# A fused attention, mixer and MLP kernel: a load pool planned by its real addresses, another rule for who gets the shared port, and the first loads issued from two queues

## The chip, the cores and the metric

The kernel runs on one core of one Trainium2 chip. The core has a matrix engine (PE, with its weight load shown as PEld), a vector engine (DVE), an activation engine (ACT), a general engine (POOL) and a queue engine (SP) that here only issues DMAs; ACT issues some as well. The metric is the device time of one execution in microseconds (us). The kernel before took 1355.23 us, the median of three runs between 1351.61 and 1355.76.

## The reference

Three parts follow each other on eight batches of 576 tokens and 512 features. First a linear attention with 8 heads of 64: `k` and `q` are projected by `w_phi` to 128 features, the row maximum of the absolute values is taken off, and both signs go through an exponential.

```
phi(x):  p = x @ w_phi; p -= max|p|; return [exp(p), exp(-p)]
kv = phi(k)^T v;  z = sum phi(k);  x = (phi(q) kv) / (phi(q) z + 1e-6)
```

Then a gated mixer and, at last, a Fourier mixing with a layer norm and an MLP:

```
gate = sigmoid(causal conv of 5 taps over x);  val = x @ w_val
x = (gate * val) @ w_out
u = x + Re(fft over tokens (fft over features (x)))
un = (u - mean) / sqrt(var + 1e-6)
out = u + max(un @ w_ch1, 0) @ w_ch2        # 512 -> 2048 -> 512
```

All inputs are fp32 but for the weights of the mixer and the MLP, which are fp64 bit patterns converted on the chip.

## The kernel before, in words

**Precision.** A product in nearly full fp32 is made of three fp32r products (`mm3`, lines 109 to 113): each operand is split into a high part (ACT, `hi_act`) and the rest, the low part (`lo_dve` on DVE or `lo_pool` on POOL). So most tiles cost one ACT and one DVE or POOL instruction. DVE and POOL read SBUF over a port that they share.

**Stages.** The attention (about 0 to 310 us) is written in a fixed order by hand (`run_attention`): 16 units of two batches by two heads, five groups each. `load_kq` and `load_v` bring a unit in; the first unit's `k` and `q` come in three pieces each. From then on a planner sets the order. `note_mix` (some 310 to 640 us) and `note_mlp` (to the end) only note operations with what they read and write; `place_ops` gives each a due time, then places them one after the other, always the one that can start first on its engine, and emits the result as five parts in time.

**The mixer**, batch by batch b = 0 to 7: `note_x` splits the attention's output `x`, `note_taps` makes the convolution and gate, `note_V` multiplies by `w_val` (PE `val`, then DVE `gv` and `gs`, then the split `ge`). `note_W` multiplies by `w_out` for four feature blocks c in the order 0, 2, 1, 3 (PE `ps<-ge,wo`, 96 matmuls for a batch). The parts are kept in `x2` (`x2b` for the last batch), and for c = 2 and 3 the difference `fs` is split into `f` (high part on ACT, low part on POOL). `note_FD` is the Fourier product over features (PE `ps<-ft,f`, result `Y` and `rem`), `note_SD` that over tokens (PE `ps<-sq,Y`), after which `u` goes to DRAM (`u_scr`). Here W(7), FD(5) and so on name such a step of batch 7 or 5.

**The MLP** works on five blocks of tokens of two halves of 462. A one-level Strassen scheme needs seven operand tiles `un` (0 to 6, each a high part `un,i,0` and a low part `un,i,1`) and seven sums of each weight, which POOL makes in the tile `ws` beforehand (`note_sums`, 16 steps). The ring `r0` (10 tiles) and `r1` (6) hold weights on their way from DRAM (`s_scr`). Three PE products per step write banks `x`, `y`, `z` and two others, `cx`, `cy`, collect the second layer in `acc`.

**The crossing from mixer to MLP.** The first block's layer norm is done during the mixer (`ln0`, in the tile `A`: two halves, three steps each) and stored to `un_scr0` and `un_scr1`. `load_first` loads the four parts from there into the low tiles of `un` 0, 6, 2 and 1, and `prep_un` (from line 795) makes the rest by subtractions on DVE or POOL (`A<-un,un` is the first, from `un` 6 and `un` 0). The tiles `un`, `r0`, `c11`, `c12`, `c22` stand in a pool (`open_mlp`) over memory that other pools held before. The list `LX` (lines 564 and 565) is their order in memory; `OLD` (from line 567) is the planner's table of what held that memory and what must be done first; `over` looks a tile up in it. The waits that the program really makes come from the addresses, not from that table.

**The port in the planner.** `free["x"]` is the time from which the shared port is free. An operation that may run on DVE or POOL ("vp") is offered to POOL unless line 1239 forbids it.

Of the kernel before, what the change touches and what calls it, by code (L numbers as in the profile page):

```python
# [13 lines left out]
ACTF = mybir.ActivationFunctionType  # L14
# [51 lines left out]
def attention_moe_mixer_kernel(  # L66
# [163 lines left out]
    def load_kq(u):  # L230
        t = P["g1"].tile([128, 2, 2 * S], F32, tag=f"g{u % 2}", name="kqraw")
        cuts = (0, 256, 640, 2 * S) if u == 0 else (0, 2 * S)
        for c0, c1 in zip(cuts, cuts[1:]):
            for w, src in enumerate((k, q)):
                nc.sync.dma_start(out=t[:, w, c0:c1], in_=src[u, :, c0:c1])
        raw[u] = [t]

    def load_v(u):
# [305 lines left out]
    def seq_pass(p, main, rem, a):  # L544
# [5 lines left out]
        else:  # L550
# [10 lines left out]
    ops = []  # L561
    ring = None

    LX = [("un", 3, 0), ("un", 3, 1), ("un", 4, 0), ("un", 4, 1), "c11", ("un", 0, 1), ("un", 6, 1), "c12", ("un", 0, 0), ("un", 6, 0), ("un", 1, 0),
          ("un", 2, 0), ("un", 5, 0), ("un", 5, 1), "c22"] + [("r0", i) for i in (3, 4, 5, 6, 7, 8, 9, 0, 1, 2)] + [("un", 2, 1), ("un", 1, 1)]
    LX_SHAPE = {"un": [2, HB], "r0": [2, 2, 128], "c11": [HB], "c12": [HB], "c22": [HB]}
    OLD = [(8192, [("done", "V", n) for n in range(2)])] * 2 + [(4 * (S + 4) * 4, [("done", "x", b)]) for b in (NB - 2, NB - 1)]
    OLD += [(4 * S * 4, OLD[0][1])] * 2 + [(4 * S + 8 * NE + 16 * NE + 8 * S - 4 * S, [("done", "g", m) for m in (2, 3)])]
    OLD += [(16 * 4 * NE, [("done", "W", c, a) for c in range(4) for a in range(2)])]

    def over(*tiles):

        keys = []
        at = 0
        for t in LX:
            n = LX_SHAPE[t if isinstance(t, str) else t[0]]
            size = -(-4 * n[0] * (n[1] if len(n) > 1 else 1) * (n[2] if len(n) > 2 else 1) // 64) * 64
            if t in tiles:
                o = 0
                for m, k in OLD:  # L580
                    if o < at + size and at < o + m:
                        keys += [x for x in k if x not in keys]
                    o += m
            at += size
        return keys
# [364 lines left out]
    def note_W(b, c):  # L950
        gh, gl = (later(("ge", b % 2, k)) for k in range(2))
        w = int(b == NB - 1)
        t = later(("x2", w))
        fs, f = tl["fs"], [later(("f", i)) for i in range(2)]
        for a in range(2):
            k, p = next(ring)
            p = p[:, 0:NE]

            def prod(e, a=a, p=p):
                for kk in range(4):  # L960
                    ws = slice(c * 128, (c + 1) * 128)
                    mm3(p, (wo[0][:, kk, ws], wo[1][:, kk, ws]), (gh[:, kk, a], gl[:, kk, a]), kk == 0, kk == 3)
            op("m", 0, prod, [("ge", b % 2, kk, i) for kk in range(4) for i in range(2)] + ["wo"], [k] + [("done", "W", c, a)] * (b == NB - 2), 12 * 0.134)
            if c >= 2:
                o_tt("v", fs[:, a], t[:, c - 2, a], p, (ALU.add, ALU.subtract)[a], NE, [k, ("x2", w, c - 2, a)], [("fs", a)])
            if c == 2 and a == 0:
                r = later(("xr", b % 2))
                o_hi(r[0:1], p[0:1], NE, [k], [("xr", b % 2, 0)])
                o_lo("v", r[32:33], p[0:1], r[0:1], NE, [k, ("xr", b % 2, 0)], [("xr", b % 2, 1)])
            o_act(t[:, c, a], p, ACTF.Copy, NE, [k], [("x2", w, c, a)])  # L970
        if c >= 2:
            c0 = c - 2
            fk = [("fs", 0), ("fs", 1)]
            o_hi(f[0][:, c0], fs, 2 * NE, fk, [("f", c0, 0)])
            o_lo(K["t_lo"], f[1][:, c0], fs, f[0][:, c0], 2 * NE, fk + [("f", c0, 0)], [("f", c0, 1)])
        if c == 2:
            q0 = 32 * (b % 4)
            o_act(later("r256")[q0:q0 + 1], t[0:1, 2], ACTF.Copy, 2 * NE, [("x2", w, 2, 0), ("x2", w, 2, 1)], [("r256", b % 4)])
# [79 lines left out]
    def note_mix():  # L1058
        rings = [[(("ps", i), later(("ps", i))) for i in range(n)] for n in (4, 5)]
        nonlocal ring  # L1060
        ring = cycle(rings[0])
        sums = iter(range(len(wsteps)))
        SUMS = [(1, 0, 1, 0, 1)] * 5 + [(1, 0, 0, 0, 0), (0,) * 5]

        def add_sums(n):
            for i in range(n):
                k = next(sums, None)
                if k is not None:
                    in_place(note_sums, k)

        ln0 = chain(ln_first(0), ln_first(1))
        tail = note_tail()
        next(tail)
        for m in range(4):
            note_taps(0, m)
            note_V(0, m)
            next(tail, None)
        for b in range(NB - 1):
            note_x(b + 1)
            for i, c in enumerate((0, 2, 1, 3)):  # L1080
                if i < 3:
                    note_taps(b + 1, i)
                    note_V(b + 1, i)
                note_W(b, c)
                add_sums(SUMS[b][i])
            add_sums(SUMS[b][4])
            note_taps(b + 1, 3)
            note_V(b + 1, 3)
            if b == NB - 2:
                ring = cycle(rings[1])  # L1090
                break
            note_FD(b)
            note_SD(b)
            for k in range((0, 1, 1, 2, 1, 1, 0)[b]):
                in_place(next, ln0, None)
        drain(ln0)
        b = NB - 2
        for n in range(RING[0]):
            note_weights(0, n)
        load_first()  # L1100
        note_FD(b)
        for c in (0, 2, 1, 3):
            note_W(b + 1, c)
        note_SD(b)
        note_FD(b + 1)
        note_SD(b + 1)
        prep_un(0, K["un0"])
# [30 lines left out]
    def place_ops():  # L1138
# [89 lines left out]
        for _ in range(n):  # L1228
            best = None
            for e, q in ready.items():  # L1230
                cand = []
                for i in q:
                    d = ops[i][0]
                    if any(left_by[e][:max(part[i], at_part[e])]):
                        continue
                    t = first(i, e)
                    if e == "p" and "v" in d:
                        ahead = sum(ops[j][0]["v"] for j in ready["v"] if j != i and due[j] <= due[i] and at[j] <= t + 0.5)
                        if t + d["p"] > max(max(free["v"], at[i]) + ahead + d["v"], due[i] + behind + d["v"] - K["marg"]):
                            continue  # L1240
                    cand.append((i, t))
                if not cand:
                    continue
                t0 = min(t for i, t in cand)
                i, t0 = min(((i, t) for i, t in cand if t <= t0 + K["win"]), key=lambda c: (due[c[0]], c[0]))
                if best is None or t0 < best[0]:
                    best = t0, e, i
            t0, e, i = best
            for q in ready.values():
                q.discard(i)  # L1250
            part[i] = at_part[e] = max(part[i], at_part[e])
            for j in succ[i]:
                part[j] = max(part[j], part[i])
            for k in ops[i][0]:
                left_by[k][last[i]] -= 1
            free[e] = t0 + ops[i][0][e]
            if e == "p" or e == "v" and ops[i][5]:
                free["x"] = free[e]
            if e == "a":
                table = ops[i][8] or table  # L1260
            if e == "m":
                behind = t0 - due[i]
            start[i], end[i] = t0, free[e] + ops[i][4]
            if ops[i][10]:
                free["w"] = max(free["w"], free[e]) + K["bw"] * ops[i][10]
                end[i] = free["w"] + K["dl"]
            order.append((i, e))
            for s in succ[i]:
                at[s] = max(at[s], end[i] + lat * ("m" not in ops[i][0] or "m" not in ops[s][0]))
                left[s] -= 1  # L1270
                if not left[s]:
                    enter(s)
# [141 lines left out]
            place_ops()  # L1414

    if True:
        nc.vector.memset(eps, 1e-6)
        nc.scalar.activation(out=warm, in_=eps, func=ACTF.Exp)
        nc.sync.dma_start(out=wp[0:64], in_=w_phi)
        nc.sync.dma_start(out=wp[64:128], in_=w_phi)  # L1420
        load_kq(0)
        nc.sync.dma_start(out=ident, in_=ident_in)
        load_v(0)
        nc.vector.memset(f32(ones), 1.0 / DM)
# [104 lines left out]
```

## Time and profile before

| what | value |
|---|---|
| median of three runs | 1355.23 us |
| the profiled execution, its own time | 1354.46 us |
| its span, first to last instruction | 1352.7 us |
| PE busy | 1307.7 us, 97% |
| DVE busy | 1178.4 us, 87% |
| ACT busy | 918.9 us, 68% |
| POOL busy | 822.2 us, 61% |

The span is what the instructions cover; 1.76 us of the execution's time lie around it. A busy share is a mean over stages: PE may be full in one and wait in the next. In the table of stretches the column PEclk is the clock granted to the matrix engine as a share of full speed; 1.00 is 2.4 GHz and 0.50 the lower level of 1.2 GHz, on which a matmul takes twice as long and the engine still counts as busy.

### The profile page before, as it was taken

Reading aid. Unit: us, or ns where it says so; the run is one execution under the profiler, and the core shown is the slowest. Engines: PE = TensorE matmul, PEld = TensorE weight load, DVE = VectorE, ACT = ScalarE, POOL = GpSimd, SP = SyncE. Lnnn points to the kernel's source line nnn. Section 1 sums busy time; section 2 is a strip of 40 time slices with the busy share of each in tenths; the row PEclk is TensorE's granted clock in tenths of the full one; section 3 lists DMA queues with packets and bytes.
Section 4 is the critical chain, followed back from the end, with each engine's and each line's share of the span. In section 5 each row is a group of like instructions: output and inputs, shape, how many; then the busy total and the mean of one; then the engine's idle time right before and its main releaser. Section 6 shows DMA issues by size and latency. Waiting matters only on the chain.

```text
span 1352.7 us, 30778 instructions
## 1 busy us (share of the span) xinstructions
PE 1307.7 (97%) x11952; PEld 1193.7 (88%) x11952; DVE 1178.4 (87%) x1867; ACT 918.9 (68%) x1872; POOL 822.2 (61%) x653
## 2 busy tenths in 40 slices
PE   7899999998999999989999999999999999999998
PEld 7788888987999999988888888888888888888997
DVE  6989988889898999869988999899988978998775
ACT  6888888866455555555877676776778676766662
POOL 4979798805666655525555765677657866673431
PEclk9999999999999999989999999999999999999999
DMA  7488888643343333243733473347333653346332
GB/s 255 143 267 263 285 280 298 209 175 130 126 141 134 127 126 133 96 154 125 236 103 106 134 231 104 102 134 237 104 108 105 211 160 102 107 112 204 103 90 87
DMA packets 151598, 214.63 MB, mean 159 GB/s; under 512 B 16790, under 2 KB 112278, under 8 KB 151452
## 3 DMA queue, kind: packets, MB, share of 16 engines
q1 hardware_dynamic: 147216, 203.21, 47.1%
q10 hardware_dynamic: 4236, 9.45, 1.8%
q8 instruction: 94, 1.54, 0.5%
q14 instruction: 52, 0.43, 0.1%
HBM read 165.63 MB, written 46.99 MB: 157 GB/s over the span
## 4 chain that ended last, share of the span: by engine, by line
PE 68%; DVE 22%; ACT 4%; issue 2%; DMA 2%; POOL 1%; SPq 0%; ACTq 0%; DVEq 0%; POOLq 0%
PE x L62 12%; PE cx L62 12%; PE cy L62 9%; PE ps L62 7%; PE y L62 6%; PE val L62 6%; DVE acc L62 4%; PE kv L62 4%; PE pj L62 4%; PE nm L62 3%; PE z L62 3%; PE yt L314 2%; DVE h L62 1%; DVE y L264 1%; DVE r L62 1%
## 5 line engine op out<-in xcount | busy, mean ns | idle before, releaser
L62 POOL TENSOR_TENSOR r<-r 128x256 fp32r<-128x256 f32 (+1 forms) x299 | 283.6, 966 | 214.3 <-ACT r L62 187.8
L62 ACT ACTIVATE r<-r 128x256 fp32r<-128x256 f32 (+1 forms) x420 | 193.0, 487 | 49.9 <-DMA r<-s_scr 48.4
L62 PE MATMUL x<-un,r 128*128 128x462 f32 (+1 forms) x960 | 223.0, 373 | 1.9 <-ACT c L62 1.9
L62 PE MATMUL cx<-h,r 128*128 128x462 f32 (+1 forms) x960 | 214.1, 371 | 3.5 <-DVE acc L62 3.5
L62 PEld LDWEIGHTS cx<-h,r 128*128 128x128 f32 x960 | 180.0, 188 | 25.6 <-DVE acc L62 5.2
L62 PEld LDWEIGHTS x<-un,r 128*128 128x128 f32 x960 | 180.7, 189 | 23.5 <-ACT c L62 2.6
L62 PE MATMUL cy<-h,r 128*128 128x462 f32 (+1 forms) x720 | 160.1, 371 | 0.0
L62 PEld LDWEIGHTS cy<-h,r 128*128 128x128 f32 x720 | 135.4, 188 | 15.2
L62 PE MATMUL val<-xh,wv 128*128 128x290 f32 x768 | 117.8, 302 | 7.4 <-DVE gv L62 3.8
L62 PEld LDWEIGHTS val<-xh,wv 128*128 128x128 f32 x768 | 108.6, 192 | 10.0 <-DVE gv L62 4.9
L62 PE MATMUL ps<-ge,wo 128*128 128x290 f32 x768 | 110.0, 301 | 6.2 <-DVE Y L62 5.4
L62 PE MATMUL y<-un,r 128*128 128x462 f32 (+1 forms) x480 | 114.4, 373 | 0.7 <-DVE h L62 0.7
L62 PEld LDWEIGHTS ps<-ge,wo 128*128 128x128 f32 x768 | 106.8, 193 | 6.6 <-DVE Y L62 5.7
L62 DVE SCALAR_TENSOR_TENSOR acc<-xf,cw,acc 128x576 f32<-128x576 f32 x128 | 105.1, 825 | 7.7 <-ACT acc L62 6.7
L62 PEld LDWEIGHTS y<-un,r 128*128 128x128 f32 x480 | 90.7, 190 | 11.7 <-DVE h L62 1.0
L261 DVE TENSOR_REDUCE m<-pj 128x8 f32<-128x1024 f32 (+1 forms) x80 | 88.7, 1108 | 12.2 <-PE pj L62 12.2
L62 ACT ACTIVATE h<-z 128x462 fp32r<-128x462 f32 (+1 forms) x120 | 66.3, 552 | 48.5 <-DVE z L62 44.0
L62 DVE TENSOR_TENSOR acc<-cx,acc 128x924 f32<-128x924 f32 (+1 forms) x80 | 88.7, 1109 | 11.7 <-PE cx L62 9.8
L62 PE MATMUL kv<-vraw,ke 128*64 128x66 f32 x2560 | 94.4, 226 | 2.0 <-DMA vraw<-in_v_dram 1.5
L62 DVE TENSOR_TENSOR r<-r 128x256 fp32r<-128x256 f32 (+1 forms) x121 | 78.9, 669 | 18.6 <-ACT r L62 18.4
L62 PE MATMUL pj<-wp,kqraw 64*128 64x128 f32 x1152 | 88.6, 291 | 5.3 <-DMA kqraw<-in_k_dram 4.5
L62 PEld LDWEIGHTS kv<-vraw,ke 128*64 128x64 f32 x2560 | 82.5, 138 | 12.7 <-ACT qe L317 1.7
(179 smaller groups left out, 2898.4 us busy)
## 6 DMA issues: line engine op xcount, KB each, us to landing
r<-s_scr SPq DMA_DIRECT2D x280, 128.0 KB, 2.1
r<-s_scr SPq DMA_DIRECT2D x140, 256.0 KB, 2.7
raw<-in_w_ch_dram SPq DMA_DIRECT2D x32, 512.0 KB, 4.8
vraw<-in_v_dram SPq DMA_DIRECT2D x16, 660.0 KB, 8.1
x_scr<-xT SPq DMA_DIRECT2D x32, 288.0 KB, 5.6
xf<-x_scr SPq DMA_DIRECT2D x8, 1152.0 KB, 9.0
u_scr<-u ACTq DMA_DIRECT2D x8, 1152.0 KB, 4.4
kqraw<-in_k_dram SPq DMA_DIRECT2D x15, 576.0 KB, 6.7
```

Of the source, the lines that this page charges most:

```text
L62: return lambda *a, **k: f(*(resolve(x) for x in a), **{n: resolve(x) for n, x in k.items()})
L261: nc.vector.tensor_reduce(out=m, in_=pv, axis=AX.X, op=ALU.max, apply_absolute_value=True)
L264: nc.vector.tensor_tensor(out=y, in0=pv, in1=m.unsqueeze(3).to_broadcast([128, 2, 2 * n, F]), op=ALU.subtract)
L314: nc.tensor.transpose(t[:, h, j, :], y[:, h, n + j, :], ident)
```

## The change

There are six edits, in the order of the file: the first `q` piece is issued by ACT instead of SP; `LX` has another order and `OLD` another content, with sizes rounded to 32 instead of 64 bytes; the copies into `x2b` name the last weight sum as a predecessor; the steps of `ln0` are spread over the batches as 0, 2, 1, 2, 1, 0, 0 instead of 0, 1, 1, 2, 1, 1, 0; POOL gets a free operation only where it would end no later than DVE would, and among operations that can start at the same time the one whose engine and inputs were ready first goes first; and `w_phi` and the first unit are issued ahead of the table load on ACT, the second copy of `w_phi` by ACT.

```
-                nc.sync.dma_start(out=t[:, w, c0:c1], in_=src[u, :, c0:c1])
+                (nc.scalar if w == 1 and u == 0 and c0 == 0 else nc.sync).dma_start(out=t[:, w, c0:c1], in_=src[u, :, c0:c1])
...
-    LX = [("un", 3, 0), ("un", 3, 1), ("un", 4, 0), ("un", 4, 1), "c11", ("un", 0, 1), ("un", 6, 1), "c12", ("un", 0, 0), ("un", 6, 0), ("un", 1, 0),
...
+    LX = [("un", 0, 1), ("un", 6, 1), ("un", 2, 1), "c11", ("un", 0, 0), ("un", 6, 0), ("un", 2, 0), ("un", 3, 0), ("un", 3, 1), ("un", 4, 0),
...
-    OLD = [(8192, [("done", "V", n) for n in range(2)])] * 2 + [(4 * (S + 4) * 4, [("done", "x", b)]) for b in (NB - 2, NB - 1)]
...
+    OLD = [(13008, [("done", "W", c, a) for c in range(4) for a in range(2)]), (11640, [("done", "g", m) for m in (2, 3)]), (8 * 4 * S, V_DONE)]
+    OLD += [(16 * (S + 4), [("done", "x", b)]) for b in (NB - 1, NB - 2)] + [(16384, V_DONE)]
...
-            o_act(t[:, c, a], p, ACTF.Copy, NE, [k], [("x2", w, c, a)])
+            o_act(t[:, c, a], p, ACTF.Copy, NE, [k] + [("s",) + wsteps[-1]] * w, [("x2", w, c, a)])
...
-            for k in range((0, 1, 1, 2, 1, 1, 0)[b]):
+            for k in range((0, 2, 1, 2, 1, 0, 0)[b]):
...
-                        if t + d["p"] > max(max(free["v"], at[i]) + ahead + d["v"], due[i] + behind + d["v"] - K["marg"]):
+                        if t + d["p"] > max(free["v"], at[i]) + ahead + d["v"]:
...
-                if best is None or t0 < best[0]:
-                    best = t0, e, i
-            t0, e, i = best
+                asked = max(free[e], at[i])
+                if best is None or (t0, asked) < best[0]:
+                    best = (t0, asked), e, i
+            (t0, _), e, i = best
...
+        for i in range(2):
+            (nc.sync, nc.scalar)[i].dma_start(out=wp[64 * i:64 * i + 64], in_=w_phi)
+        load_kq(0)
         nc.vector.memset(eps, 1e-6)
         nc.scalar.activation(out=warm, in_=eps, func=ACTF.Exp)
-        nc.sync.dma_start(out=wp[0:64], in_=w_phi)
-        nc.sync.dma_start(out=wp[64:128], in_=w_phi)
-        load_kq(0)
```

The attention's instructions keep their order; everything from the planner on is dealt anew. Three places follow.

SP's queue at the crossing, before. `un_0_1` is the low tile of `un` 0, `un_scr1_74` the second half's store, `ws` and `s_scr` the weight sums.

```order
L679 DMA s_scr1_3_86<-ws_5722 128x4x256 [waits DMAHW2_49,Pool_49]
L679 DMA un_0_1_8738<-un_scr0_73 128x924 [waits DVE_49,Activation_49]
L679 DMA un_scr1_74<-A_115 128x1848 [waits DMAHW6_49]
L679 DMA un_1_1_8759<-un_scr0_73 128x924 [waits PE_49]
L679 DMA r0_1_8756<-s_scr0_0_75 128x256
L679 DMA r0_2_8757<-s_scr0_0_75 128x256
L679 DMA un_6_1_8739<-un_scr1_74 128x924 [waits DMAHW6_49,DVE_49,Pool_49]
L679 DMA un_2_1_8758<-un_scr1_74 128x924 [waits DMAHW3_49]
```

And now:

```order
L679 DMA un_scr1_74<-A_115 128x1848 [waits DMAHW3_49,DVE_49]
L679 DMA s_scr1_3_86<-ws_5722 128x4x256 [waits DMAHW2_49,Pool_49]
L679 DMA r0_0_8751<-s_scr0_0_75 128x256 [waits Activation_49]
L679 DMA r0_1_8752<-s_scr0_0_75 128x256
L679 DMA r0_2_8753<-s_scr0_0_75 128x256
L679 DMA r0_8_8750<-s_scr0_1_76 128x256 [waits DMAHW1_49,DVE_49,Activation_49]
L679 DMA r0_9_8749<-s_scr0_1_76 128x256
L679 DMA un_0_1_8734<-un_scr0_73 128x924 [waits DMAHW3_49,PE_49]
L679 DMA un_6_1_8735<-un_scr1_74 128x924 [waits DMAHW4_49]
L679 DMA un_2_1_8736<-un_scr1_74 128x924 [waits DMAHW5_49]
```

The store to `un_scr1` has moved ahead of the last weight sum and of all loads of `un`, and the first load of `un` waits for PE instead of DVE and ACT.

DVE around the last two differences `fs` that FD(5) needs, before (`sl` and `s` are of the layer norm, `A` its tile):

```order
L62 TENSOR_TENSOR sl_6078<-s_114,sh_6073 128x462
L62 TENSOR_TENSOR xh<-xf,xh 128x576 x2
L62 TENSOR_TENSOR fs<-x_6065,ps_6082 128x290
L62 SCALAR_TENSOR_TENSOR acc<-xf,cw,acc 128x2x288 x2
L62 TENSOR_TENSOR fs<-x_6065,ps_6083 128x290
```

And now:

```order
L62 RECIPROCAL s_114<-s_114 128x116
L62 RECIPROCAL s_114<-s_114 128x114
L62 TENSOR_TENSOR A<-A,s_114 128x924 x2
L62 TENSOR_TENSOR fs<-x_6062,ps_6080 128x290
L62 TENSOR_TENSOR fs<-x_6062,ps_6081 128x290
```

The layer norm's last step has come forward to this place; the splits of `x` and the taps have left it (the four splits of batch 6 are POOL's now).

PE from the end of SD(6) on, before (`ps_6083` and `ps_6084` are banks of the mixer, `x` and `y` of the MLP):

```order
L62 MATMUL ps_6083<-sr,rem_6072 128x290 x2
L62 MATMUL x_8730<-un_0_8741,r_0_8755 128x462
...
L62 MATMUL ps_6084<-sq,Y_6070 128x290 x2
...
L62 MATMUL y<-un_0_8735,r_1_8756 128x462
...
L62 MATMUL z<-un_0_8743,r_3_8748 128x462
...
L62 MATMUL ps_6085<-ft_107,f_6069 128x258
```

And now:

```order
L62 MATMUL ps_6080<-sr,rem_6069 128x290 x2
L62 MATMUL ps_6082<-ft_107,f_6066 128x258
L62 MATMUL ps_6082<-ft_108,f_6066 128x258
L62 MATMUL ps_6082<-ft_107,f_6071 128x258
...
L62 MATMUL x_8731<-un_0_8738,r_0_8751 128x462
```

The three first MLP products (18 matmuls), which stood between SD(6) and FD(7), now follow SD(7).

## Rows read from the trace of the kernel before

**Rows 1.** The page: busy time, share of the span, instructions.

```profile
PE 1307.7 (97%) x11952; PEld 1193.7 (88%) x11952; DVE 1178.4 (87%) x1867; ACT 918.9 (68%) x1872; POOL 822.2 (61%) x653
```

**Rows 2.** Stretches: span, length; busy PE, PEld, DVE, ACT, POOL; PEclk, DMA, GB/s.

```profile
312.00:552.00 240.00, 229.15 (x1791) 224.00 (x1789) 219.55 (x407) 132.97 (x268) 143.84 (x131) 0.99 0.39 133
552.00:595.00 43.00, 41.17 (x299) 40.51 (x299) 32.49 (x60) 20.12 (x46) 15.92 (x15) 0.96 0.30 103
595.06:600.50 5.44, 0.01 (x2) 0.00 (x1) 1.48 (x3) 2.02 (x4) 0.26 (x1) 0.87 0.96 341
600.50:612.62 12.12, 12.12 (x72) 12.12 (x73) 11.62 (x14) 10.32 (x24) 7.59 (x4) 0.78 0.16 52
645.00:1348.00 703.00, 698.80 (x3328) 624.47 (x3326) 613.31 (x867) 486.38 (x1015) 418.78 (x394) 1.00 0.45 136
...
740.00:800.00 60.00, 58.47 (x277) 51.28 (x276) 56.28 (x72) 41.68 (x87) 42.46 (x38) 1.00 0.62 195
```

**Rows 3.** PE's waits (line waited for: us, times, longest).

```profile
PE ps L62 <- DVE Y L62: 5.4, 1, 5.4
...
PE pj L62 <- DMA kqraw<-in_k_dram: 4.5, 1, 4.5
...
PE ps L62 <- ACT f L62: 1.6, 1, 1.6
...
PE ps L62 <- POOL f L62: 1.0, 1, 1.0
```

**Rows 4.** Timeline of the start: start, duration, instruction.

```profile
0.73 0.59 SPq L1419 DMA_DIRECT2D wp<-in_w_phi_dram  x1
...
2.00 0.58 SPq L235 DMA_DIRECT2D kqraw<-in_k_dram  x1
```

**Rows 5.** Timeline around FD(5), DVE.

```profile
547.09 2.66 DVE L62 TENSOR_TENSOR xh<-xf,xh 128x576 fp32r<-128x576 f32 x2
...
550.04 1.67 DVE L62 SCALAR_TENSOR_TENSOR acc<-xf,cw,acc 128x576 f32<-128x576 f32 x2
...
551.62 0.45 DVE L62 TENSOR_TENSOR fs<-x,ps 128x290 f32<-128x290 f32 x1
```

**Rows 6.** Timeline at the crossing: layer norm, end of W(6), first load.

```profile
580.64 1.63 DVE L62 TENSOR_TENSOR A<-A,s 128x924 f32<-128x924 f32 x1
...
583.83 3.38 PE L62 MATMUL val<-xh,wv 128*128 128x290 f32 x24
...
588.84 0.33 SPq L679 DMA_DIRECT2D un<-un_scr  x1
```

**Rows 7.** Chain that ended last, at the crossing.

```profile
589.22 6.14 DMA un_scr<-A
...
595.43 3.53 DMA un<-un_scr
```

**Rows 8.** Timeline, PE: W(7), SD(6), first product of FD(7).

```profile
600.50 12.29 PE L62 MATMUL ps<-ge,wo 128*128 128x290 f32 x72 [5.43 <-DVE Y L62]
...
613.56 0.96 PE L62 MATMUL ps<-sq,Y 128*128 128x290 f32 x6
...
617.47 1.08 PE L62 MATMUL ps<-sq,Y 128*128 128x290 f32 x6 [0.35 <-DVE fs L62]
...
621.04 0.90 PE L62 MATMUL ps<-ft,f 128*128 128x258 f32 x6
```

**Rows 9.** Instruction groups by shape (busy us, mean ns).

```profile
L62 POOL TENSOR_TENSOR f<-fs,f 128x580 fp32r<-128x580 f32 x16 | 24.4, 1527 | 36.9 <-ACT f L62 36.6 <-POOL u L62 0.3
...
L62 POOL TENSOR_TENSOR A<-B,A 128x924 f32<-128x924 f32 x3 | 6.0, 2016 | 2.3 <-DVE A L62 2.3
...
L62 DVE RECIPROCAL s<-s 128x116 f32<-128x116 f32 x30 | 26.0, 867 | 0.1
...
L62 DVE TENSOR_TENSOR A<-B,A 128x924 f32<-128x924 f32 x3 | 5.2, 1742 | 0.0
...
L62 DVE TENSOR_TENSOR s<-s,A 128x462 f32<-128x462 f32 x4 | 2.9, 714 | 0.0
```

More of the change, by code (lines that the diff above doesn't have):

```diff
@@ L562, in attention_moe_mixer_kernel @@
     ring = None
-    LX = [("un", 3, 0), ("un", 3, 1), ("un", 4, 0), ("un", 4, 1), "c11", ("un", 0, 1), ("un", 6, 1), "c12", ("un", 0, 0), ("un", 6, 0), ("un", 1, 0),
-          ("un", 2, 0), ("un", 5, 0), ("un", 5, 1), "c22"] + [("r0", i) for i in (3, 4, 5, 6, 7, 8, 9, 0, 1, 2)] + [("un", 2, 1), ("un", 1, 1)]
+    LX = [("un", 0, 1), ("un", 6, 1), ("un", 2, 1), "c11", ("un", 0, 0), ("un", 6, 0), ("un", 2, 0), ("un", 3, 0), ("un", 3, 1), ("un", 4, 0),
+          ("un", 4, 1), ("un", 5, 0), "c12", "c22", ("un", 5, 1)] + [("r0", i) for i in (9, 8, 0, 1, 2)] + [("un", 1, 1)] + [("r0", i) for i in (3, 4, 5, 6, 7)] + [("un", 1, 0)]
     LX_SHAPE = {"un": [2, HB], "r0": [2, 2, 128], "c11": [HB], "c12": [HB], "c22": [HB]}
-    OLD = [(8192, [("done", "V", n) for n in range(2)])] * 2 + [(4 * (S + 4) * 4, [("done", "x", b)]) for b in (NB - 2, NB - 1)]
-    OLD += [(4 * S * 4, OLD[0][1])] * 2 + [(4 * S + 8 * NE + 16 * NE + 8 * S - 4 * S, [("done", "g", m) for m in (2, 3)])]
-    OLD += [(16 * 4 * NE, [("done", "W", c, a) for c in range(4) for a in range(2)])]
+    V_DONE = [("done", "V", n) for n in range(2)]
+    OLD = [(13008, [("done", "W", c, a) for c in range(4) for a in range(2)]), (11640, [("done", "g", m) for m in (2, 3)]), (8 * 4 * S, V_DONE)]
+    OLD += [(16 * (S + 4), [("done", "x", b)]) for b in (NB - 1, NB - 2)] + [(16384, V_DONE)]
     def over(*tiles):
@@ L576, in over @@
             n = LX_SHAPE[t if isinstance(t, str) else t[0]]
-            size = -(-4 * n[0] * (n[1] if len(n) > 1 else 1) * (n[2] if len(n) > 2 else 1) // 64) * 64
+            size = -(-4 * n[0] * (n[1] if len(n) > 1 else 1) * (n[2] if len(n) > 2 else 1) // 32) * 32
             if t in tiles:
```

## The prediction

> **What bounds the kernel now.** I read the page's engine line first: PE is busy 1307.7 of 1352.7 us, 97% [rows 1]. So at most 45 us can be won on PE's waits, and in addition what PE loses at the lower clock while it counts as busy. Second I read where PE stands still. The list of its waits names four places that the change touches: 5.4 us before W(7) for `Y` on DVE, 4.5 us at the start for the first `k`, and 1.6 and 1.0 us in FD(5) for the two halves of `f` [rows 3]. Third come the stretches [rows 2]. The mixer up to FD(5), 312 to 552, has 240 − 229.15 = 10.85 us of PE idle, with DVE at 219.55 of 240: there DVE is nearly as full as PE, so any new deal of its work moves small PE waits. The MLP, 645 to 1348, has only 703 − 698.80 = 4.2 us of PE idle, with DVE idle for 90 us: nothing is to be won there, something may be lost.
>
> The largest wait is read along its chain [rows 6, 7]. The layer norm's last `A*s` ends at 580.64 + 1.63 = 582.27, but its store to `un_scr1` starts only at 589.22, since SP's queue has a load of `un` ahead of it that waits for DVE and ACT and goes out at 588.84. The store lands at 595.36, the load behind it takes 3.53, to 598.96, and then DVE does `A<-un,un`, behind which `Y` stands in DVE's queue. PE waits from 595.06 to 600.50. Behind the wait PE's clock is low: between 600.50 and 612.62 the granted clock is 0.78 and W(7)'s 72 matmuls take 12.12 us [rows 2]. At full clock a W matmul takes 3.38/24 = 0.141 us by the `val` products of the same width [rows 6], 72 take about 10.1. I count 2.0 for the clock.
>
> **The start: −0.9.** One of the two slots ahead of the first `k` on SP goes to ACT. `k` is issued 2.00 − 0.73 = 1.27 behind the first `w_phi`, that is 0.64 a slot [rows 4]. So `k` is asked for 0.64 earlier, and everything behind the first `q` piece 1.27 earlier, as that piece has left SP too. ACT's table load now runs after two issues, under the 4.5 us in which PE waits for `k` anyway [rows 3]. From below the gain is nothing, if the transfers and not the asking set when `k` and `q` are there; from above it is 1.27. I take 0.9, between one slot and two. The Trainium skill ("DMA: Bandwidth & Descriptors", "Issuing engines are not separate DMA queues") says that asking from several engines saves only the time that it takes to ask, as all share the same 16 DMA engines; by that the start gives one slot and the sum is 0.3 higher.
>
> **FD(5) and the mixer up to it: −2.0.** Before, DVE put two splits of `x` (2.66), two taps (1.67) and an `sl` ahead of the last `fs` at 551.62 [rows 5]; then came `fs` 0.45, ACT's half of `f`, and POOL's half of 1.53 [rows 9], and PE waited 1.6 + 1.0 for these two [rows 3]. Behind it stands a clock of 0.96 over 43 us, at 0.04 × 43 = 1.7 [rows 2]. Now the splits of this batch are POOL's, nothing stands between the last two `fs`, and ahead of them are two reciprocals of 0.87 [rows 9] and two `A*s` of at most 1.63 [rows 6], 5.0 in all against some 5.7 before. The best is that both waits and the clock go, 2.6 + 1.7 = 4.3. The worst is not measured by any row of before: the layer norm's steps now fall into other batches, POOL's ones change, and DVE's idle in this stretch is 20.45 us, against 10.85 of PE [rows 2]. If the new deal is worse by a quarter of what PE already loses there, it is +3. Of the two ends I stay nearer to the one with rows, and take half the best, −2.0.
>
> **The crossing: −7.0.** Three things are changed. The store to `un_scr1` stands before every load of `un` in SP's queue, and `A*s`, on which it waits, is made a batch earlier, near FD(5). So it is long done when the loads are due. The new addresses put `un` 0, 6 and 2 over memory of which the loads wait for PE's last W(6) product alone (the order shows PE as the waited engine). W(6) ends where the `val` products begin, 583.83 [rows 6]. Loads issued then, the low tiles of 0 and 6 behind each other, take 3.53 [rows 7] and an issue slot of some 0.3 to 0.6 each, and are there by 588 to 589. DVE reached its place for `A<-un,un` only after the load, at 599, with `Y` due before 595; so the wait of 5.44 goes whole, and with it the 2.0 for the clock and the 0.35 in SD(6) [rows 8]: 7.8 at best.
>
> What is late next is the path from W(7) to FD(7). Before, three MLP products of 6 matmuls lay beside it; now they come after SD(7), and only SD(6) does, with 30 matmuls of 0.141, 4.2 in all (six of them take 0.96 with the pipeline's end [rows 8]). The path from W(7)'s last product is `fs` 0.45 [rows 5], ACT's half of `f`, which I put at no more than 0.8 by POOL's 1.53 for the same tile, and POOL's half [rows 9], some 2.8: covered, if DVE and ACT come to it at once. They may not: with W(7) at full clock, 10.1 us, ACT's 10.32 us of work [rows 2] is longer than the stretch. The bound on that side: before, FD(7) began at 621.04 [rows 8], 8.4 behind W(7)'s end at 600.50 + 12.12, without a wait for `f`. So the path took no more than 8.4, and if it took all of that, 8.4 − 4.2 = 4.2 of it now lies bare. So the crossing lies between −7.8 and −3.6. Since DVE loses the subtractions of the crossing from its queue ahead of `fs`, I take a stall of 0.8, that is −7.0.
>
> **The MLP: 0.** POOL's new rule gives operations back to DVE. By the order, DVE gains five `A` differences and sums, seven of the `s` operations net of those it loses, and one `sl`. At 1.74 for `A` and 0.71 for `s` [rows 9] these are 8.7 + 5.0 = 13.7, nearly all in the four changes of block, 3.4 each. From 740 to 800, one such change, DVE has 60 − 56.28 = 3.72 idle and PE waits 1.53 [rows 2]. So the work just fits, and I price it at 0; at best PE's 4.2 go, at worst all 13.7 are added. The zero is the nearer: where POOL did the same operation it took 2.02, so DVE gets the result sooner than by handing it over. The port speaks for it as well: the Trainium skill ("SBUF — State Buffer", "Who interferes with whom") says that DVE and POOL hold their shared port pair exclusively, and the loser stands still for the whole instruction. By that a POOL operation of 2.02 cost DVE as much as doing it, and rival C below would have no price; the row's idle time cannot show which it is.
>
> Nothing is counted for the copies into `x2b`, whose new predecessor, the last weight sum, is stored long before W(7) at 600.50 writes them.
>
> **Sum.** 1354.46 − 0.9 − 2.0 − 7.0 + 0 = 1344.6 for the profiled execution, which stands 0.77 below the median of the runs; on the median's scale 1345.3, so 1345.
>
> **The rivals.** About 0.3%, 4.1 us, is what a measurement of this kernel can tell from no change; faster is below 1351.2 here.
>
> A. The crossing gives what I say, but the new deal before FD(5) gives back +4 instead of −2: 1345.3 + 6 = 1351.3, on the border. For it: DVE is 91% busy there, and every place of an operation is new. Against: DVE's work does not grow, and the named wait gets shorter.
>
> B. The wait is only turned into another: FD(7) now waits 4.2 for `f`, the crossing gives 3.6, and the mixer +2 instead of −2: 1345.3 + 3.4 + 4.0 = 1352.7, the same. For it: ACT's 10.32. Against: the path of 2.8 under 4.2 of SD(6).
>
> C. Slower: DVE's added 3.4 us a block change isn't covered. The price decides where DVE's idle in a change (3.72) is already needed for PE's results; then the layer norm's whole 13.7 stands on PE: 1345.3 + 13.7 = 1359.0. Against: 90 us of DVE idle over the MLP, and work that may slip past the change.
>
> D. More is won: both waits at FD(5) and the clock go (−4.3), the crossing gives 7.8, the start 1.27, and 3 of the mixer's other waits: 1345.3 − 2.3 − 0.8 − 0.4 − 3 = 1338.8.
>
> **Chances and range.** The forecast 0.56, from 1341 to 1350; D 0.10; A 0.14, half of it on either side of the border; B 0.12; C 0.08. Faster: 0.56 + 0.10 + 0.07 + 0.01 of C half paid = 0.74. Same: 0.07 of A and 0.10 of B = 0.17. Slower: 0.07 of C and 0.02 of B, where the mixer loses more = 0.09. The range takes D's 1338 and reaches past B, to 1355; outside it stay C and what lies below D, under 2 in 10.
>
> **What would show it.** In the changed kernel's trace the store of `un_scr1` should start before any load of `un`, and the first load of `un` right behind the last W(6) product. PE should have no wait of some microseconds before W(7), and a granted clock near 1.00 in it. The wait before FD(7) is then the term to measure: below 1 by the forecast, 4.2 by B. In FD(5) PE's waits for `f` should be below 2.6, with the idle from the start of the mixer to FD(5) near 9 or 10; 15 would be A. The first product should start 0.6 to 1.3 earlier. In the MLP PE's idle should stay near 4.2; waits for DVE in the four block changes would be C. The forecast is wrong if the load of `un` still waits for something later than W(6), or if the waits of the newly dealt mixer add up to more than the crossing wins.

## The result, and the profile after

The changed kernel took 1339.91 us (median of four runs, 1338.95 to 1343.12) beside 1353.42 for the kernel before; the ratio is 0.9909, with a 95% interval of 0.9882 to 0.9936. At the measured ratio that is 12.3 us, where 9.9 were forecast. The time lies in the range of 1338 to 1355, just under the 1341 to 1350 of the forecast itself, and it is not made of the terms of the sum.

The profiled execution took 1343.12 with a span of 1341.3, 11.4 us shorter than the span before. I cut both at four points of PE's timeline: the first `val`, the end of W(6), the end of W(7) and the last product. The table gives each stage's length, and in brackets how long PE stood still in it. Length less idle is PE's busy time for the same work; where that differs, I put it down to the clock.

| kernel | to first `val` | mixer, to end of W(6) | crossing, to end of W(7) | to last product |
|---|---|---|---|---|
| before | 313.6 | 270.4 (12.5) | 28.8 (5.4) | 735.2 (6.6) |
| changed | 314.0 | 271.7 (12.2) | 20.7 (0.0) | 730.2 (4.6) |

So the crossing gave 8.1 us (5.4 of waiting, 2.6 of clock), the MLP side 5.0 (2.0 of waiting, 3.0 of clock), and the mixer lost 1.3, with 0.3 less of waiting and 1.7 more of busy time. The rows of PE's waits in the changed kernel (line waited for: total, times, longest) answer to [rows 3]:

```profile
PE pj L62 <- DMA kqraw<-in_k_dram: 4.5, 1, 4.5
PE val L62 <- DVE gv L62: 4.0, 7, 2.0
PE val L62 <- DVE gs L62: 3.1, 5, 1.8
...
PE x L62 <- ACT c L62: 1.4, 1, 1.4
...
PE cx L62 <- DVE acc L62: 1.1, 2, 0.5
```

And three of the kernel before:

```profile
PE val L62 <- DVE gv L62: 3.8, 5, 1.3
PE cx L62 <- DVE acc L62: 3.5, 4, 1.6
...
PE val L62 <- DVE gs L62: 0.7, 2, 0.3
```

The 5.4 for `Y` and the 2.6 for `f` are gone; the 4.5 at the start are not. `gv` and `gs`, 4.5 together before, are 7.1: the mixer's waits have moved. The timeline at the crossing answers to [rows 7, 8]:

```profile
555.99 0.33 SPq L679 DMA_DIRECT2D un_scr<-A  x1
...
585.74 3.40 SPq L679 DMA_DIRECT2D un<-un_scr  x4
...
592.19 0.75 DVE L62 TENSOR_TENSOR Y<-ps,Y 128x258 fp32r<-128x258 f32 x2
592.86 1.11 DVE L62 TENSOR_TENSOR A<-un,un 128x924 f32<-128x924 f32 x1
...
593.40 13.04 PE L62 MATMUL ps<-ge,wo 128*128 128x290 f32 x96
```

The store goes out at 556, the loads of `un` at 585.74, 0.03 behind the end of W(6), and W(7) runs its 96 products in 13.04 us with nothing in front. One more thing is new here: the last `Y` stands ahead of `A<-un,un` on DVE, where in the kernel before it stood behind it:

```profile
598.99 1.12 DVE L62 TENSOR_TENSOR A<-un,un 128x924 f32<-128x924 f32 x1 [8.09 <-DMA un<-un_scr]
600.03 0.42 DVE L62 TENSOR_TENSOR Y<-ps,Y 128x258 fp32r<-128x258 f32 x1
```

The stretches of W(7) and of the rest answer to [rows 2] (span, length, busy time and count of PE, PEld, DVE, ACT, POOL, then PEclk, DMA, GB/s):

```profile
593.40:606.45 13.05, 13.05 (x100) 13.05 (x99) 12.55 (x12) 12.26 (x30) 9.96 (x6) 1.00 0.06 19
606.45:645.00 38.55, 36.39 (x213) 33.18 (x213) 35.62 (x61) 23.98 (x55) 22.45 (x20) 1.00 0.60 204
645.00:1336.00 691.00, 688.60 (x3286) 617.38 (x3285) 605.36 (x867) 482.52 (x1001) 402.31 (x377) 1.00 0.45 134
730.00:790.00 60.00, 60.00 (x288) 53.84 (x287) 57.47 (x78) 45.06 (x92) 41.47 (x39) 1.00 0.62 200
```

PEclk is 1.00 in W(7), against 0.78 behind the wait before. In the MLP, from 645 to 1336, PE is idle for 2.4 us, where it was 4.2 [rows 2]. In a change of block DVE has 57.47 of 60 busy and PE none idle.

### The profile page after: what moved, and what is told of

Read it like the earlier page. It is cut to its first block, busy times and chain, and to the rows that moved or that the text cites. A ratio compares the mean times of both kernels' runs of the same rounds, so it can differ in the third digit from the quotient of the medians.

```text
span 1341.3 us, 30805 instructions
## 1 busy us (share of the span) xinstructions
PE 1303.6 (97%) x11952; PEld 1190.6 (89%) x11952; DVE 1175.5 (88%) x1879; ACT 926.1 (69%) x1874; POOL 812.9 (61%) x641
## 4 chain that ended last, share of the span: by engine, by line
PE 81%; DVE 10%; DMA 3%; POOL 2%; ACT 2%; issue 1%; SPq 0%; DVEq 0%; POOLq 0%; ACTq 0%
PE x L62 15%; PE cx L62 14%; PE cy L62 11%; PE ps L62 10%; PE y L62 7%; PE kv L62 5%; PE pj L62 4%; PE val L62 4%; PE nm L62 4%; PE z L62 4%; PE yt L314 2%; DVE acc L62 2%; POOL ws L62 1%; DVE m L261 1%; DVE y L264 1%
## 5 line engine op out<-in xcount | busy, mean ns | idle before, releaser
L62 POOL TENSOR_TENSOR r<-r 128x256 fp32r<-128x256 f32 (+1 forms) x301 | 293.1, 990 | 243.5 <-ACT r L62 224.7
L62 PE MATMUL nm<-kvT,qe 128*64 128x65 f32 x2304 | 83.4, 223 | 7.5 <-DVE xs L343 5.1
```

What stands on the lines that cost most here:

```text
L62: return lambda *a, **k: f(*(resolve(x) for x in a), **{n: resolve(x) for n, x in k.items()})
```

## The experiments

Several edits had changed at once, so I took them apart. Each ratio is to the kernel before, run beside it; mixer, crossing and the rest are lengths from one profile each, cut as above, with PE's idle time in brackets.

| label | edits in it | median | ratio, 95% | mixer | crossing | to last product |
|---|---|---|---|---|---|---|
| e1 | start | 1351.78 (one run) | | 271.9 (13.0) | 28.5 (5.3) | 733.8 (6.8) |
| e2 | addresses, norm's spread | 1347.28 | 0.9954, 0.9936 to 0.9972 | 270.8 (12.3) | 20.7 (0) | 734.4 (6.6) |
| e3 | POOL's rule, asking | 1355.54 | 1.0019, 1.0003 to 1.0034 | 271.9 (12.1) | 28.6 (5.0) | 736.2 (8.4) |
| e4 | addresses | 1345.28 | 0.9937, 0.9920 to 0.9954 | 269.3 (12.0) | 20.7 (0) | 734.8 (6.9) |
| e5 | all but addresses | 1350.53 | 0.9974, 0.9959 to 0.9989 | 270.4 (11.6) | 22.5 (1.5) | 741.8 (10.0) |
| e6 | all but norm's spread | 1339.67 | 0.9892, 0.9878 to 0.9905 | 271.6 (13.2) | 20.7 (0) | 729.0 (3.4) |
| e7 | all but POOL's rule | 1347.54 | 0.9947, 0.9935 to 0.9960 | 270.6 (12.5) | 20.7 (0) | 735.2 (6.9) |
| e8 | all but asking | 1339.99 | 0.9896, 0.9881 to 0.9912 | 266.7 (9.3) | 20.7 (0) | 732.6 (5.3) |
| e9 | POOL's rule | 1344.70 | 0.9922, 0.9902 to 0.9942 | 261.6 (6.7) | 28.5 (5.4) | 733.4 (5.5) |
| e10 | addresses, POOL's rule | 1338.34 | 0.9874, 0.9847 to 0.9900 | 263.0 (7.1) | 20.7 (0) | 734.5 (5.6) |
| e11 | asking from W(7) on, first `q` on SP | 1337.63 | 0.9862, 0.9833 to 0.9891 | 268.4 (11.0) | 20.7 (0) | 728.9 (3.3) |
| e12 | as e11, old spread, `w_phi` on ACT | 1330.38 | 0.9827, 0.9801 to 0.9852 | 261.7 (6.6) | 20.7 (0) | 728.9 (3.3) |

How far one profile can be trusted, the traces tell: in five groups of kernels PE, DVE, ACT and POOL run the same instructions in the same order through the mixer. They took 270.4, 271.9 and 269.3 us (before, e1, e4), 261.6, 263.0 and 261.7 (e9, e10, e12), 271.9 and 271.6 (e3, e6), 266.7 and 268.4 (e8, e11), 271.7 and 270.4 (the changed kernel, e5). So a mixer's length in one profile stands for its kernel within some 2.6 us.

**The start alone (e1).** These lines of the change, with `w_phi` and the first loads ahead of the table load:

```
+                (nc.scalar if w == 1 and u == 0 and c0 == 0 else nc.sync).dma_start(out=t[:, w, c0:c1], in_=src[u, :, c0:c1])
...
+            (nc.sync, nc.scalar)[i].dma_start(out=wp[64 * i:64 * i + 64], in_=w_phi)
```

> The kernel before with the two edits of the start alone (first q piece and second w_phi copy issued by ACT, table load behind them). Theory T1 (from the changed kernel's trace): asking earlier does not bring k earlier, because the first q piece now travels beside it and both share the transfer's throughput; PE's first product starts at 4.5 us again, only the first v (PE kv) comes 0.4 earlier, and the end moves by less than 1 us. Rival R1 (the prediction's term): PE starts 0.6 earlier and the end moves by 0.9; then the wait at 4.5 in the changed kernel had another cause.

PE's first product started at 4.55, so T1 holds for `k`. The one run, 1351.78, lies inside the spread of the kernel before, and says nothing of the end.

**Addresses with the layer norm's spread (e2), and without (e4).** e2 takes `LX`, `OLD`, the rounding, the predecessor of `x2b` and this line; e4 leaves the line out:

```
-            for k in range((0, 1, 1, 2, 1, 1, 0)[b]):
+            for k in range((0, 2, 1, 2, 1, 0, 0)[b]):
```

> The kernel before with the new addresses (LX, OLD, rounding), the predecessor of the x2b copies and the new spread of the layer norm's steps; planner rules and start as before. Theory T1: nearly the whole gain of the mixer's end is here: PE waits less than 1 us before W(7), the clock in W(7) is 1.00, and the time falls by 8 to 10 us, ratio 0.993 to 0.994. Rival R2: the gain comes from the new rules of the planner (which deal all of the mixer and MLP anew), and this alone gives 0 to 4 us, ratio 0.997 to 1.000.

> The kernel before with the new addresses and the predecessor of the x2b copies alone, the layer norm's steps spread as before. By the order of its instructions the store to un_scr1 already stands ahead of all loads of un, and the first load waits for PE. Theory T1a: the addresses are enough for the crossing: A*s ends at 582, the store lands near 588.5, the load near 592, and PE waits less than 1 us before W(7); what the layer norm's spread adds is at FD(5) (waits of 2.6 us stay here). Time 6 to 8 us below, ratio 0.994 to 0.996. Theory T1b: the layer norm's step must come a batch earlier as well; then PE still waits 2 us or more before W(7), ratio above 0.996.

e4's ratio is a little below T1a's range, and e2's above T1's. In both the crossing takes 20.7 us and PE waits for nothing in it, so the addresses, with the predecessor of `x2b`, are enough (T1a), and R2 falls as an account of the crossing. A kernel with new addresses differs here in two things, as the planner works from them: the loads go out right behind W(6), and the last `Y` no longer stands behind `A<-un,un` on DVE. No run has one without the other.

**The two rules of the planner alone (e3).** The lines in `place_ops`:

```
+                        if t + d["p"] > max(free["v"], at[i]) + ahead + d["v"]:
...
+                asked = max(free[e], at[i])
+                if best is None or (t0, asked) < best[0]:
```

> The kernel before with the two new rules of the planner alone (POOL only where it ends no later than DVE; who asked first goes first). Theory T1: the wait of 5 us before W(7) stays, since the store to un_scr1 still stands behind the first load of un in SP's queue; the MLP's waits change by a few us, and the time falls by 0 to 4 us, ratio 0.997 to 1.000. Rival R2: it falls by 8 or more (ratio below 0.994). Rival C of the prediction: more work on DVE makes it slower, ratio above 1.003.

The wait of 5.0 stays, as T1 says, but nothing is won: at 1.0019 it is slightly slower. The MLP proper is better, the steps at its beginning worse (6.1 us of waits for `c` before 646), and the mixer no better.

**The store's place against the addresses (e5).** `LX`, `OLD`, the rounding and the predecessor of `x2b` are taken back to the kernel before:

```
-    LX = [("un", 0, 1), ("un", 6, 1), ("un", 2, 1), "c11", ...
+    LX = [("un", 3, 0), ("un", 3, 1), ("un", 4, 0), ("un", 4, 1), "c11", ...
...
-            o_act(t[:, c, a], p, ACTF.Copy, NE, [k] + [("s",) + wsteps[-1]] * w, [("x2", w, c, a)])
+            o_act(t[:, c, a], p, ACTF.Copy, NE, [k], [("x2", w, c, a)])
```

> The changed kernel with the old addresses and without the predecessor of the x2b copies. By the order of its instructions the store to un_scr1 stands ahead of all loads of un here, but the first load waits for DVE and ACT as in the kernel before. It tells the store's place from the addresses. Theory T2a (the store behind the load was the whole of the 5.4 us): the load goes out near 589 and its 3.5 us end near 593, PE waits less than 1.5 us before W(7), and the mixer's crossing from the end of W(6) to that of W(7) takes 21 to 22 us. Theory T2b (the load's own wait counts as much): PE still waits 2.5 us or more, the crossing takes 24 or more. In both the time lies between the two kernels, ratio to before 0.992 to 0.998.

The load went out at 586.67, `A<-un,un` at 592.89, and PE waited:

```profile
594.40 1.86 PE L62 MATMUL ps<-ge,wo 128*128 128x290 f32 x12 [1.52 <-DVE Y L62]
```

`Y` stands behind `A<-un,un` here, as before. With the store ahead of the loads 3.9 of the 5.4 us go, and 1.5 stay with the load's own wait: T2a's mechanism, by a hair over its bounds (the crossing takes 22.5). So the time at which the load is there sets the wait. Whether earlier loads would have taken the last 1.5 without the new place of `Y` isn't tried. By an estimate they would: in e6 the tiles 0 and 6 landed 3.5 and 4.6 behind W(6), DVE came to this place at 6.8, and 1.1 for `A<-un,un` would put the end of `Y` near 8.4, where PE asks for it near 11.0. Behind the crossing e5 takes 11.6 more than the changed kernel, with waits of 5.6 for `c` and 2.9 for `fs`: beside the two rules of the planner the new addresses gave more there than in the crossing.

**All but the new spread (e6), all but POOL's rule (e7), all but the order of asking (e8).**

In each the hunk that is shown elsewhere for it is taken back; for e8 this one:

```
-                asked = max(free[e], at[i])
-                if best is None or (t0, asked) < best[0]:
-                    best = (t0, asked), e, i
-            (t0, _), e, i = best
+                if best is None or t0 < best[0]:
+                    best = t0, e, i
+            t0, e, i = best
```

> The changed kernel with the layer norm's steps spread as before. Theory T3: the new spread only moves waits of the mixer (the 2.6 us at FD(5) come back and waits of val for gv and gs go), so this one is as fast as the changed kernel or 1 to 2 us faster, ratio to before 0.988 to 0.991; the crossing from W(6) to W(7) stays at 20.8 us. Rival (the prediction's step on FD(5)): it is 2 us slower than the changed kernel, ratio 0.992 or more.

> The changed kernel with the old rule for when POOL gets an operation (who asked first goes first stays). With the new addresses alone PE waited 0.9, 0.7 and 1.5 us for acc in the MLP, with the two new rules together these waits are mostly gone. Theory T4a: the rule for POOL does it; here the waits for acc come back, the stretch from the end of W(7) to the last product takes 734 us instead of 730, ratio to before 0.993 to 0.995. Theory T4b: the order of asking does it; here the stretch takes 730 to 731 and the ratio is 0.990 to 0.992.

> The changed kernel without the order of asking (POOL's new rule stays). Theory T4a: the stretch from the end of W(7) to the last product takes 730 to 731 us, ratio to before 0.990 to 0.992. Theory T4b: it takes 734, ratio 0.993 to 0.995.

e6 is as fast as the changed kernel: the rival falls, the new spread gives nothing beside the other edits. But it is not so in T3's way: with the old spread PE waits 0.8 for `f`, not 2.6, and 9.3 for `gv` and `gs`, not less. e7 loses 5.0 of the stretch to the last product: T4a in its numbers, but not in its path. The waits for `acc` stay at 1.1, as in the changed kernel; PE's idle time is 2.4 longer, 1.1 of it for `Y` and 1.1 for `h`, and its busy time 2.6. e8 was to tell the same and did not: its end takes 732.6, between the theories, and its mixer 266.7, 5 less than with the order of asking. That was in neither theory, and the last four runs were chosen for it.

**POOL's rule alone (e9), and with the addresses (e10).**

```
-                        if t + d["p"] > max(max(free["v"], at[i]) + ahead + d["v"], due[i] + behind + d["v"] - K["marg"]):
+                        if t + d["p"] > max(free["v"], at[i]) + ahead + d["v"]:
```

> The kernel before with POOL's new rule alone (old addresses, old order of asking, old start, old layer norm spread). With the new addresses the rule was worth some 6 us, together with the order of asking on the old addresses it gave nothing. Theory T5a: it is the order of asking that lost it there (a mixer 4 to 5 us longer than without it); then the rule alone gives about as much on the old addresses: mixer from its first val to the end of W(6) 267 us, ratio 0.994 to 0.997. Theory T5b: it is the old addresses: with u_scr stored 8 us later, the loads of acc from u_scr wait in SP's queue with the weights behind them, and PE waits 5 us or more for c between 630 and 650; then the rule alone gives nothing here either, ratio 0.998 to 1.002.

> The kernel before with two of the six edits: the new addresses (with the predecessor of the x2b copies) and POOL's new rule. Theory T6: these two are the whole gain, ratio 0.988 to 0.991, as fast as the changed kernel; the start, the layer norm's spread and the order of asking are worth nothing together. Rival: the other three are worth 2 us or more, ratio 0.992 or above.

This one line shortens the mixer by 8.8 us, more than T5a said, and T5b falls. e10 is at least as fast as the changed kernel, at the lower end of what T6 said: the start, the new spread and the order of asking together give nothing. The mixer's stretch in e9, and then in e3, which differ by the order of asking alone:

```profile
314.30:576.00 261.70, 255.03 (x1975) 249.57 (x1972) 247.23 (x468) 147.14 (x298) 137.16 (x130) 1.00 0.39 133
```

```profile
312.10:583.90 271.80, 259.67 (x1972) 252.77 (x1971) 243.53 (x456) 148.57 (x298) 155.20 (x142) 0.99 0.39 128
```

And the kernel before:

```profile
314.00:584.00 270.00, 257.50 (x1971) 252.31 (x1970) 246.72 (x454) 146.49 (x297) 156.92 (x144) 0.99 0.38 129
```

POOL's rule takes 14 operations from POOL (144 to 130) and gives them to DVE (454 to 468), and DVE's busy time rises by no more than 0.5 us. PE's idle time over the whole mixer falls by 5.8 and its busy time, for the same work, by 2.9, which I put down to the clock (1.00 against 0.99). Ten of the 14 are low parts of `ge`; on DVE they take 7.9 us before, then in e9 14.4:

```profile
L62 DVE TENSOR_TENSOR ge<-gs,ge 128x580 fp32r<-128x580 f32 x8 | 7.9, 986 | 0.2
```

```profile
L62 DVE TENSOR_TENSOR ge<-gs,ge 128x580 fp32r<-128x580 f32 x18 | 14.4, 801 | 0.9 <-ACT ge L62 0.8
```

The order of asking gives 12 of the 14 back to POOL, and with them all of the gain. DVE's load does not explain that, since DVE is less busy in e3 than in e9 (243.5 against 247.2). What differs is what waits on whom: in e3 POOL has 24 of the 32 low parts `xh`, in e9 17, and PE's waits for `gv` and `gs` are 8.6 against 4.6. The code says how this may come about: when DVE and POOL could both start at the time the port comes free, DVE, which stands first in the list of engines, went first; by the order of asking the one that was ready earlier goes first. That it is this, and not some other tie, was not tried by itself.

**The order of asking from W(7) on (e11, e12).** The two lines that they share, and what e12 has beyond (it takes the old spread too):

```
-                asked = max(free[e], at[i])
+                asked = max(free[e], at[i]) if at_part['m'] >= 3 else 0.0
...
-                (nc.scalar if w == 1 and u == 0 and c0 == 0 else nc.sync).dma_start(out=t[:, w, c0:c1], in_=src[u, :, c0:c1])
+                nc.sync.dma_start(out=t[:, w, c0:c1], in_=src[u, :, c0:c1])
```

```
-            (nc.sync, nc.scalar)[i].dma_start(out=wp[64 * i:64 * i + 64], in_=w_phi)
+            nc.scalar.dma_start(out=wp[64 * i:64 * i + 64], in_=w_phi)
```

> The changed kernel with two edits. The order of asking decides only from the part of the program that opens with W(7) on (before it the planner takes the older rule, as in the kernel without the order of asking). And the first q piece goes back to SP, behind the first k, while the second w_phi stays with ACT. Theory T7: the mixer is 267 us from its first val to the end of W(6) and the stretch from the end of W(7) to the last product 730, so 3 to 5 us faster than the changed kernel, ratio 0.986 to 0.988. On the start, theory T1: with nothing beside it k lands 0.6 earlier and PE starts at 3.9 instead of 4.5. Rival R1: PE starts at 4.4 to 4.5 again, then not the q piece held k back.

> As the kernel before this one, with the layer norm's steps spread as in the kernel before, and with both halves of w_phi issued by ACT, so that k is the first on SP. Theory T1: k lands 1.2 earlier than in the changed kernel, but the second w_phi, on ACT's second slot, lands near 3.6 and then sets the start: PE at 3.6 to 3.9. Rival R1: PE at 4.4 to 4.5 again. The rest as theory T7, ratio 0.986 to 0.988; if the older spread costs the mixer anything with this rule, 0.988 to 0.990.

T7 holds for the end: 728.9 us in both. The mixer is 268.4 with the new spread of the layer norm and 261.7 with the old: without the order of asking the new spread costs 6.7 (by e8 and e10, 3.7). I had not foreseen that, and e12, at 0.9827, is faster than any ratio that I gave for it. It beats both kernels, by 1.7% to the kernel before. On the start, the first product of e11:

```profile
1.38 0.83 SPq L235 DMA_DIRECT2D kqraw<-in_k_dram  x1
2.26 0.43 SPq L235 DMA_DIRECT2D kqraw<-in_q_dram  x1
...
4.01 1.23 PE L62 MATMUL pj<-wp,kqraw 64*128 64x128 f32 x8 [4.01 <-DMA kqraw<-in_k_dram]
```

`k` is asked for at 1.38 as in the changed kernel, without `q` beside it, and PE starts at 4.01 instead of 4.51: T1. In e12 `k` goes out at 0.74:

```profile
3.18 0.79 PE L62 MATMUL pj<-wp,kqraw 64*128 64x128 f32 x2 [3.18 <-DMA wp<-in_w_phi_dram]
...
4.66 0.58 PE L62 MATMUL pj<-wp,kqraw 64*128 64x128 f32 x2 [0.69 <-DMA wp<-in_w_phi_dram]
```

PE starts at 3.18, and then stands until the second half of `w_phi` is there at 4.66, where I had expected that at 3.6 to 3.9: beside `k` and `q` that half took 3.3 us from issue to landing, in the changed kernel 2.2.

**Where the MLP side's 5 us come from.** The stretch takes 729 to 730 where POOL's rule, the new addresses and the order of asking come together (changed kernel, e6, e11, e12), 733 to 735 without the order of asking (e8 to e10) and 735 without POOL's rule (e7). I cut it once more, behind the first 200 products that follow W(7):

| kernels | first 200 products | the rest |
|---|---|---|
| without POOL's rule (before, e1, e2, e4, e7) | 37.1 to 39.3 | 695.8 to 696.9 |
| with it, but without the addresses or the order of asking (e3, e5, e8, e9, e10) | 40.4 to 48.7 | 692.2 to 694.4 |
| with all three (changed, e6, e11, e12) | 36.1 to 36.2 | 692.8 to 694.0 |

Before and now, the two stretches are:

```profile
612.79:651.07 38.28, 35.90 (x201) 32.30 (x201) 33.63 (x59) 21.53 (x53) 17.34 (x15) 0.96 0.56 185
651.07:1347.96 696.89, 692.72 (x3299) 619.03 (x3298) 607.82 (x858) 480.58 (x1003) 415.03 (x391) 1.00 0.45 134
```

```profile
606.45:642.60 36.15, 33.99 (x201) 31.04 (x201) 33.22 (x57) 22.60 (x53) 21.02 (x18) 1.00 0.57 193
642.60:1336.63 694.03, 691.63 (x3299) 619.73 (x3298) 607.76 (x871) 483.89 (x1003) 403.73 (x378) 1.00 0.45 135
```

So 2.1 of the 5.0 us lie ahead of the MLP proper, nearly all in busy time at a clock of 0.96 against 1.00, and 2.9 in it, 1.8 of waits and 1.1 of busy time. In the MLP proper POOL's rule gives that in every kernel that has it. Ahead of it the rule alone costs time, and the three edits together gain. In e10 the three first MLP products still stand inside SD(6), and PE waits there:

```profile
607.53 1.63 PE L62 MATMUL ps<-sq,Y 128*128 128x290 f32 x6 [2.30 <-DVE fs L62]
```

DVE did the differences of `un` first and came to the last two `fs` at 607.03, 7.4 behind W(7)'s end at 599.64. In the changed kernel the products follow SD(7), and the last `fs` come at the end of W(7):

```profile
606.07 0.86 DVE L62 TENSOR_TENSOR fs<-x2b,ps 128x290 f32<-128x290 f32 x2
```

## Why the prediction was right, and where it was not

**The crossing, −7.0: right in mechanism and nearly in size.** The chain was as read: a store held up in SP's queue by a load that waits, then 6 and 3.5 us of transfers. All 5.44 went (e2, e4, e6 to e8, e10 to e12), with the load going out right behind W(6). The clock behind it was worth 2.6, not 2.0. Of the three things that I named, the `A*s` made a batch earlier wasn't needed (e4), and the place of the store was worth 3.9 by itself (e5). That `Y` would go ahead of `A<-un,un` I had not seen. The stall of 0.8 that I put ahead of FD(7) did not come: PE waits for nothing between 606 and 629. I had the three MLP products as cover that goes; in e10, where they stand inside SD(6), DVE does their `un` ahead of `fs`, and PE waits 2.3 for it.

**FD(5) and the mixer, −2.0: wrong.** The step that failed is "nothing stands between the last two `fs`, and ahead of them are two reciprocals": I priced the named wait, which did go, and credited its place with the gain. The mixer as a whole became 1.3 longer, by the means of the groups above 0.6, which is within what one deal varies by; and e6 has the same 271.6 without the new spread. The 1.7 for the clock did not hang on the wait either: e4 has the same waits and a clock of 1.00 behind them (last section). Behind that sum stand terms that I had no price for, by the means of the groups: POOL's rule −8.4, the order of asking +9.7 on top of it (+3.5 with the new spread), the new spread +5.5 where asking is off. I had only bounded the new deal as one thing, by −4.3 and +3; its parts are two to three times that and cancel.

**The MLP, 0: the gain was 5.0.** Rival C is refuted: DVE took the work and PE's waits for `acc`, 3.5 us before, fell to 1.1. The step that failed is "nothing is to be won there": of PE's idle time in the MLP proper 1.8 us went, with 1.1 of busy time. The other 2.1 lie between W(7) and the MLP proper, which the sum left out. The row that answers to [rows 9], and the same row with POOL's rule alone, in e9:

```profile
L62 DVE TENSOR_TENSOR A<-B,A 128x924 f32<-128x924 f32 x5 | 6.2, 1240 | 0.0
```

```profile
L62 DVE TENSOR_TENSOR A<-B,A 128x924 f32<-128x924 f32 x4 | 7.5, 1864 | 0.0
```

So the 1.74 of before is no price of the operation: it takes 1.24 in one deal and 1.86 in another. What a POOL operation beside it costs DVE, the crossing of the changed kernel shows, where `A<-un,un` above took 1.11:

```profile
594.21 2.18 POOL L62 TENSOR_TENSOR un<-un,un 128x924 fp32r<-128x924 f32 x1 [1.24 <-DMA r<-s_scr]
594.91 2.45 DVE L62 TENSOR_TENSOR A<-un,A 128x924 f32<-128x924 f32 x1
```

A difference of the same size takes 1.34 us longer beside POOL. That is what the Trainium skill ("SBUF — State Buffer", "Who interferes with whom") says: a DVE instruction with two inputs in SBUF contends with one of POOL that reads SBUF. The mixer's stretches agree: 14 more operations on DVE for 0.5 us. I weighed the rule only against rival C's price; it was the ground for a rival of its own, in which POOL's rule makes the mixer faster.

**The start, −0.9: not shown.** By PE's first product it gave nothing (4.49, 4.51 and, in e1, 4.55), since the first `q` piece, issued at the same time, held `k` back: `k` took 3.0 us from issue to landing, and 2.5 in e11, which shows the 0.5 that is there without it. Here the Trainium skill's sentence on issuing engines ("DMA: Bandwidth & Descriptors", "Issuing engines are not separate DMA queues") was nearer than my choice, as its point is that the transfers share the engines. Whether the later loads' lead reaches the end can't be told: to the first `val` six profiles with the old start took 312.1 to 316.0, mean 313.8, and six with the new one (before e11 and e12) 311.1 to 314.2, mean 312.4.

**The sum.** −0.9 −2.0 −7.0 + 0 was forecast; 0.4 + 1.3 − 8.1 − 5.0 = −11.4 is what the two profiles show. The crossing is foresight; that the sum comes so near is in part luck, since the misses on the start and the mixer (+1.3 and +3.3) and on the crossing and the MLP (−1.1 and −5.0) have opposite signs.

## What to carry to other kernels

Look in a queue for what is stuck behind the instruction that waits: here one load ahead of a store cost 3.9 of the 5.4 us for which PE stood still, and other addresses alone, with the order that the planner makes of them, took away all of it and the low clock behind it. When a planner's rule changes, price it by what it does to the whole stage, not by the one wait that can be named, nor by the busy time of the fullest engine alone (e3 against e9); and test each rule alone, since here two rules in one edit hid a gain of 9 us. Between two engines with one port, an operation handed to the slower engine can cost the faster one as much as doing it: here 1.34 us beside POOL's 2.18, for a size that DVE does in 1.11.

## What the runs showed of the hardware

A wait on PE does not always cost clock. The kernel before and e4 have the same two waits of 1.61 and 1.00 us at FD(5), and the same mixer, instruction by instruction; the 20 us from 550 on read, in the kernel before and in e4:

```profile
550.00:570.00 20.00, 17.39 (x120) 16.82 (x119) 17.14 (x35) 8.40 (x20) 9.95 (x11) 0.91 0.16 53
```

```profile
550.00:570.00 20.00, 17.40 (x131) 16.81 (x130) 18.25 (x36) 10.30 (x22) 11.74 (x13) 1.00 0.16 53
```

The granted clock is 0.91 in one and 1.00 in the other; in e1, again with the same mixer, it is 0.91. Over a whole execution this is a few us: length less idle of the mixer was 255.0 to 259.8 for the same work, lowest in e9 and highest in e3, and 257.3 to 258.9 for the one order of the kernel before, e1 and e4. It is part of why single profiles here differ by more than some of the edits under test.
